# Two blocks of 256 tokens at a time in a fused attention and mixture-of-experts kernel: first products of 512 columns, and a new order of the opening

## The chip, the cores and the metric

One core of a Trainium2 chip runs the whole kernel. The metric is device time in microseconds for one execution; a time given without more is the median of several. A profiled execution also has a span, from its first to its last instruction. The engines are TensorE (PE in the rows; PEld is its loading of weights), VectorE (DVE), ScalarE (ACT), GpSimd (POOL) and SyncE (SP), which issues most of the DMAs. Each engine runs its own instructions in order and waits for others by semaphores.

## What is computed

```python
B, H, S, D = (4, 8, 576, 64)      # attention: scale, two causal masks, softmax, product with v
x = attention(q, k, v)            # laid out as x[2304, 512]
h = x @ w_in                      # first layer, w_in[512, 2048]
x1 = (h * np.cos(h)) @ w_out      # w_out[2048, 512]
logits = x1 @ w_gate + np.log1p(np.exp(x1 @ w_noise)) * noise     # 8 experts
top2_w = softmax of the two largest logits of each row
out[rows] += top2_w * (np.maximum(x1[rows] @ w1[e], 0) @ w2[e])   # w1[8, 512, 1024], w2[8, 1024, 512]
```

Four heads see the last 32 positions, four see every fourth of the last 128. The inputs of the first layer and of the experts come as 64-bit floats.

## The kernel before

Numbers are carried as two parts: a high part rounded to the type that TensorE multiplies at its full rate (float32r), and the rest, the low part. Each product of two numbers is three matmuls (PASSES, line 43: high x high, high x low, low x high). Splitting a tile into its parts is two operations: a copy on ACT that rounds, and a subtraction on DVE or POOL. For weights of the first layer three operations on DVE go ahead (w_bits, lines 323 to 325, tile `cut`), which cut a 64-bit float down to 32 bits; then w_parts (lines 331 and 333) makes the parts `wm`. The set OTHER names the subtractions that are on DVE and not on POOL (`w..` those of the weights, `g..` those of g below), and the moves that are on ACT.

The tokens are nine blocks of 256, the 2,048 hidden columns eight groups of 256. A step is one block and one group:

- g1 (line 595) multiplies the split x of the block, `xhl`, with the group's weights: 24 matmuls of 256 columns (2 halves of the group x 4 chunks x 3 passes; L606) into one of two banks `ph`;
- post (line 609) makes h cos h of it: ACT, DVE (L615), ACT Sin and Square (L617, L618), DVE (L619), then the parts of g: an ACT copy (L622) and a subtraction (L624);
- g2 (line 627) multiplies the g of two steps earlier with w_out: 12 matmuls of 512 columns (L634), which are added up over the groups in two of four banks `acc`.

The 72 steps: in steps 0 to 15 blocks 0 and 1 take turns, group by group, while the weights are still being loaded and split; then blocks 2 to 8 follow, eight steps each. `xhl` has two buffers, so the next block is split (x_split, line 586) while the present one is multiplied.

In between stands all other work, in an order written out by hand. LOADS and OPENING, two strings, give the opening: loads of queries, keys and values (Q, V) and of weights (W), scores (S), exponentials (E), norms (N: L511, L512 and the scaling), transposes (T), products with v (A), weight cuts (B) and parts (P), splits of x (X), first products (G). BESIDE, a table, gives the rest: a row `20:0` says what stands in step 20 at position 0. A step's positions are -1 (after g1), 0 and 1 (after the first half of g2), 2 (after its second half). There stand the later attention units (a_...), the weights (w_...), the splits of x, and the router of each block once its first layer is done (r_rows copies x1 out, r_trans turns it, r_gate, r_logits, r_exp, r_top, r_pick, r_rank, r_send choose the experts and send the rows). Routers take their banks from `acc`, attention from two banks `mid`. At the end of the steps the work of expert 0 begins (t_..., load_we, split_we). Then the expert stage follows: for each expert, w1 (L956) and w2 (L991).

## Time and profile before

| | us |
|---|---|
| median of three runs | 998.86 (997.47 to 1001.2) |
| the profiled execution | 999.23 |
| its span | 997.4 |
| TensorE busy | 966.2 (97%) |
| VectorE busy | 531.4 (53%) |
| ScalarE busy | 459.6 (46%) |
| GpSimd busy | 339.3 (34%) |
| mean granted clock of TensorE | 0.99 |

The shares are means over stages that differ: the opening, in which attention and the splitting of the weights run, up to some 130 us; the rest of the first layer with later attention units and the routers beside it, up to 538 us; and the expert stage. In a timeline a run of equal instructions is one row, with the start of the first, the time from there to the end of the last, and their number; since the end of a matmul is modelled and the next one starts before, the time that a group takes is read from its start to the start of the next group.

### The profile page before, as it was taken

The numbers are of one execution on the slowest core, as the hardware profiler recorded it, in microseconds if no ns is written. First come the engines' busy times: TensorE is split into PE (matmuls) and PEld (weight loads), VectorE is DVE, ScalarE is ACT, GpSimd is POOL, SyncE is SP. The second block draws the span as 40 slices with busy tenths as digits, with TensorE's granted clock in tenths as the row PEclk, the third lists the DMA queues.
The fourth block names the chain that finished last, engine by engine and source line by source line (L and its number), as shares of the span: only waits on it lengthen the run. The fifth ranks groups of instructions, "written<-read, shape, count | busy, mean of one in ns | idle before, by whom it ended". The sixth has DMA issues, their size and how long they took to land.

```text
span 997.4 us, 17303 instructions
## 1 busy us (share of the span) xinstructions
PE 966.2 (97%) x6843; PEld 848.6 (85%) x6843; DVE 531.4 (53%) x1151; ACT 459.6 (46%) x919; POOL 339.3 (34%) x457
## 2 busy tenths in 40 slices
PE   8798989999999999999999999999999999999996
PEld 5677879888888888898987789898898989898995
DVE  5899774546755555344466656354453535353321
ACT  6767665555646755465464435232332414232210
POOL 6634342343353342323332232332313232322302
PEclk9999989999999999999999999999999999999999
DMA  8843221312231210000064454443434243441201
GB/s 301 304 136 107 83 84 34 122 69 73 84 77 53 67 32 1 22 7 17 1 219 110 105 174 145 155 163 124 158 122 151 85 156 136 158 158 46 80 11 61
DMA packets 52596, 104.50 MB, mean 105 GB/s; under 512 B 12483, under 2 KB 24771, under 8 KB 52512
## 3 DMA queue, kind: packets, MB, share of 16 engines
q1 hardware_dynamic: 42528, 75.68, 23.3%
q0 software_dynamic: 9984, 27.68, 9.0%
q8 instruction: 55, 0.90, 0.4%
q14 instruction: 29, 0.24, 0.1%
HBM read 84.76 MB, written 19.59 MB: 105 GB/s over the span
## 4 chain that ended last, share of the span: by engine, by line
PE 80%; DVE 10%; ACT 4%; issue 2%; DMA 2%; POOL 1%; SPq 0%; DVEq 0%; POOLq 0%; ACTq 0%
PE pe L956 21%; PE ye L991 20%; PE ph L606 16%; PE acc L634 15%; PE sc L466 2%; DVE cut L324 2%; PE mo L549 2%; PE mgx L939 2%; DVE cut L325 2%; PE mt L529 1%; DVE cut L323 1%; DVE r L615 1%; DVE r L619 1%; DMA qts<-in_qT 1%; PE mx L661 1%
## 5 line engine op out<-in xcount | busy, mean ns | idle before, releaser
L606 PE MATMUL ph<-xhl,wm 128*128 128x256 f32 x1728 | 225.4, 286 | 6.6 <-POOL wm L333 3.1
L606 PEld LDWEIGHTS ph<-xhl,wm 128*128 128x128 f32 x1728 | 217.5, 193 | 14.2 <-POOL wm L333 4.2
L634 PE MATMUL acc<-wm,g 128*128 128x512 f32 x864 | 223.4, 401 | 5.2 <-ACT wm L331 2.0
L991 PE MATMUL ye<-we,h 128*128 128x512 f32 (+1 forms) x960 | 227.4, 393 | 0.0
L991 PEld LDWEIGHTS ye<-we,h 128*128 128x128 f32 (+1 forms) x960 | 172.7, 183 | 41.1
L634 PEld LDWEIGHTS acc<-wm,g 128*128 128x128 f32 x864 | 156.3, 190 | 38.0 <-ACT wm L331 2.4
L624 POOL TENSOR_TENSOR g<-r,g 128x512 fp32r<-128x512 f32 x65 | 84.3, 1298 | 183.3 <-ACT g L622 182.9
L956 PE MATMUL pe<-xga,we 128*128 128x352 f32 x768 | 126.1, 324 | 0.0
L956 PEld LDWEIGHTS pe<-xga,we 128*128 128x128 f32 x768 | 123.2, 188 | 0.4 <-issue 0.4
L1004 POOL DMA_INDIRECT out<-old,tir x35 | 35.3, 1008 | 219.9 <-DVE old L1002 215.5
L958 ACT ACTIVATE h<-pe 128x256 fp32r<-128x256 f32 (+1 forms) x128 | 54.3, 424 | 119.5 <-PE pe L956 119.5
L959 DVE SCALAR_TENSOR_TENSOR h<-pe,h 128x256 fp32r<-128x256 f32 (+1 forms) x128 | 60.6, 475 | 86.7 <-ACT h L958 83.2
L1002 DVE SCALAR_TENSOR_TENSOR old<-ye,wts,old 128x512 f32<-128x512 f32 (+1 forms) x35 | 26.2, 750 | 133.8 <-PE ye L991 133.8
L956 PE MATMUL pe<-xgb,we 128*128 128x256 f32 x768 | 90.1, 276 | 1.7 <-DVE h L959 1.7
L615 DVE SCALAR_TENSOR_TENSOR r<-r,ph 128x512 f32<-128x512 int32 x72 | 49.2, 683 | 78.5 <-ACT r L614 78.4
L956 PEld LDWEIGHTS pe<-xgb,we 128*128 128x128 f32 x768 | 88.8, 188 | 2.2 <-DVE h L959 1.9
L872 DVE TENSOR_TENSOR we<-wraw,we 128x512 fp32r<-128x512 f32 x128 | 88.0, 698 | 4.3 <-ACT we L871 1.7
L619 DVE SCALAR_TENSOR_TENSOR r<-r,ph 128x512 f32<-128x512 f32 x72 | 49.4, 686 | 70.4 <-ACT r L618 70.4
L871 ACT ACTIVATE we<-wraw 128x512 fp32r<-128x512 f32 x128 | 78.1, 623 | 0.0
L617 ACT ACTIVATE r<-r 128x512 f32<-128x512 f32 x72 | 45.5, 632 | 54.1 <-DVE r L615 53.9
L614 ACT ACTIVATE r<-ph 128x512 int32<-128x512 f32 x72 | 42.8, 595 | 56.4 <-PE ph L606 46.7
L622 ACT ACTIVATE g<-r 128x512 fp32r<-128x512 f32 x72 | 45.5, 632 | 48.4 <-DVE r L619 38.6
(191 smaller groups left out, 980.2 us busy)
## 6 DMA issues: line engine op xcount, KB each, us to landing
wraw<-in_we SPq DMA_DIRECT2D x64, 512.0 KB, 6.1
raw<-in_wm SPq DMA_DIRECT2D x28, 512.0 KB, 8.5
x1d<-x SPq DMA_DIRECT2D x9, 512.0 KB, 3.1
out<-zt SPq DMA_DIRECT2D x18, 256.0 KB, 4.2
vts<-in_v SPq DMA_DIRECT2D x11, 384.0 KB, 3.9
kts<-in_kT SPq DMA_DIRECT2D x13, 288.0 KB, 4.5
qts<-in_qT SPq DMA_DIRECT2D x13, 288.0 KB, 4.5
piece<-in_wm SPq DMA_DIRECT2D x4, 512.0 KB, 5.1
```

What stands on the lines that cost most here:

```text
L606: nc.tensor.matmul(ph[:, j, :], w[:, a, o:o + P], t[:, x, c, :], start=(c == 0 and n == 0 and (j == 0 or len(cs) == 4)), stop=(c == 3 and ...
L615: nc.vector.scalar_tensor_tensor(r, n, -TWO_PI, ph, op0=ALU.mult, op1=ALU.add)
L617: nc.scalar.activation(r, r, AF.Sin, scale=0.5)
L619: nc.vector.scalar_tensor_tensor(r, r, 0.5, ph, op0=ALU.subtract, op1=ALU.mult)
L624: eng.tensor_tensor(g[:, 1, :], r, g[:, 0, :].bitcast(F32), op=ALU.subtract)
L634: nc.tensor.matmul(ACC[blk][t], g[:, a, j * TB + t * P:j * TB + (t + 1) * P], w[:, x, 1024 + j * DM:1024 + (j + 1) * DM], start=(p == 0 an ...
L871: nc.scalar.activation(t[:, 0, fs], raw, AF.Copy)
L872: eng.tensor_tensor(t[:, 1, fs], raw, t[:, 0, fs].bitcast(F32), op=ALU.subtract)
L956: nc.tensor.matmul(ph[:, :n], w[:, a, o:o + P], x[:, b, c, :], start=(c == 0 and i == 0), stop=(c == 3 and i == 2))
L958: nc.scalar.activation(h[:, 0, f, :n], ph[:, :n], AF.Relu)
L959: nc.vector.scalar_tensor_tensor(h[:, 1, f, :n], ph[:, :n], 0.0, h[:, 0, f, :n].bitcast(F32), op0=ALU.max, op1=ALU.subtract)
L991: nc.tensor.matmul(acc, h[:, a, f, o:o + n], w[:, b, (f % 4) * DM:(f % 4 + 1) * DM], start=(f == 0 and i == 0), stop=(f == 7 and i == 2))
```

## The change

Blocks 0 to 7 are taken in pairs. A step is now one pair of blocks (512 tokens) and one half group (128 hidden columns): 64 such steps, f = 0 to 15 for each pair, and then block 8 with its eight steps as before. g1_pair has 12 matmuls of 512 columns (4 chunks x 3 passes), whose moving operand is 256 columns of the one block and 256 of the other. g2_pair has 12 matmuls of 512 columns, as g2, over four token tiles: it fills all four banks `acc` for a pair. `xhl` is one tile with a place for either block of a pair, no longer two rotating buffers. The routers of blocks 0 to 5 take their banks from `mid`. post is the same; a piece of w_out is one half group's, so w_parts(p,3) is needed one step later than w_parts(p,2).

```diff
+0:-1 w_load(3,0)
...
-12:-1 a_norm(7)
...
-20:0 r_rows(1) x_split(3)
...
+15:-1 x_split(2,0,2) w_parts(7,2) zero_out(5)
+15:0 x_split(3,0,2) x_split(3,2,4) x_split(2,2,3,1) x_split(2,3,4,1)
...
+31:-1 a_part(11,2) x_split(4,2,4) x_split(5,2,4) x_split(4,0,2) r_send(1,1)
+31:0 x_split(5,0,2)
...
+47:-1 x_split(6,0,2) x_split(7,0,2) x_split(7,2,4) x_split(6,2,4)
...
+63:-1 x_split(8)
...
-OTHER = set("g02 g04 g07 g10 g13 g14 g15 m40 m41 m50 m51 m60 m61 m70 m71 t62 t71 w02 w12 w20 w22 w32 w33 w42 w43 w53 w61 w63".split())
+OTHER = set("e4 e7 g0_0 g0_1 g0_10 g0_11 g0_14 g0_15 g0_2 g0_3 g0_4 g0_5 g0_6 g0_7 g0_9 m40 m50 m51 m60 m61 m70 m71 n2 t62 t70 t71 w02 w10 w11 w12 w20 w22 w32 w33 w41 w43 w50 w60 w61 w63 w73".split())
...
+    xhl = bpool.tile([P, 2, 2, 4, TB], F32R, name="xhl")
     XHL = {}
...
     def x_split(blk, c0=0, c1=4, st=2, eng=nc.vector):
-        if c0 == 0:
-            XHL[blk] = bpool.tile([P, 2, 4, TB], F32R, tag="xhl", name=f"xhl{blk}", bufs=2)
-        t = XHL[blk]
+        t = xhl[:, blk % 2]
+        XHL[blk] = t
...
+    def g1_pair(b, f, cs=range(4)):
+        w = WM[f // 2]
+        if (b, f) not in PH:
+            tag, bufs = ("acc", 4) if (b, f) == (0, 1) else ("ph", 2)
+            PH[b, f] = psum.tile([P, 2 * TB], F32, tag=tag, name=f"ph{b}_{f}", bufs=bufs)
+        ph = PH[b, f]
+        for c in cs:
+            for n, (a, x) in enumerate(PASSES):
+                o = c * 256 + (f % 2) * P
+                nc.tensor.matmul(ph, w[:, a, o:o + P], xhl[:, :, x, c, :],
+                                 start=(c == 0 and n == 0), stop=(c == 3 and n == 2))
+        return ph
...
+    def g2_pair(b, f, ts):
+        g, w = G[b, f], WM[f // 2]
+        if f == 0 and 0 in ts:
+            for blk in (b, b + 1):
+                ACC[blk] = [psum.tile([P, DM], F32, tag="acc", name=f"acc{blk}_{t}", bufs=4) for t in range(2)]
+        for t in ts:
+            for n, (a, x) in enumerate(PASSES):
+                nc.tensor.matmul(ACC[b + t // 2][t % 2], g[:, a, t * P:(t + 1) * P],
+                                 w[:, x, 1024 + f % 2 * DM:1024 + (f % 2 + 1) * DM],
+                                 start=(f == 0 and n == 0), stop=(f == 2 * NPAIR - 1 and n == 2))
+
...
+    def r_bank(blk, name):
+        tag, bufs = ("mid", 2) if blk < 6 else ("acc", 4)
+        return psum.tile([P, 512], F32, tag=tag, name=name, bufs=bufs)
...
-            if blk >= NBLK - 2:
+            if blk >= NBLK - 3:
...
-    steps = [(blk, p) for p in range(NPAIR) for blk in range(2)]
-    steps += [(blk, p) for blk in range(2, NBLK) for p in range(NPAIR)]
+    steps = [(b, f) for b in (0, 2, 4, 6) for f in range(2 * NPAIR)]
+    steps += [(NBLK - 1, p) for p in range(NPAIR)]
+    paired = range(64)
```

The strings LOADS and OPENING and most rows of BESIDE are new as well. Expert 0's first gathers read the rows of blocks 0 to 5 and no longer those of block 6, and a few tiles of the expert stage have other offsets. Three places show how the order moves.

VectorE in the first 15 us: L480 and L482 (L493 and L495 after) are the score reductions `sc` and `mx` of an attention unit, L511 and L512 (L524 and L525) its norm `sm`; the first number in a name is the unit. Before:

```order
L480 TENSOR_REDUCE sc1_1_230<-sc1_1_230 128x4
L482 TENSOR_SCALAR mx1_214<-sc1_1_230 128x4
L480 TENSOR_REDUCE sc2_0_254<-sc2_0_254 128x5
L482 TENSOR_SCALAR mx2_253<-sc2_0_254 128x5
L480 TENSOR_REDUCE sc2_1_268<-sc2_1_268 128x4
L482 TENSOR_SCALAR mx2_253<-sc2_1_268 128x4
L511 TENSOR_SCALAR sm0_242<-sm0_242 128x9
L512 RECIPROCAL sm0_242<-sm0_242 128x9
L534 COPY ahat_89<-mt0_0_298 96x384
L511 TENSOR_SCALAR sm1_282<-sm1_282 128x9
L512 RECIPROCAL sm1_282<-sm1_282 128x9
```

After:

```order
L493 TENSOR_REDUCE sc1_1_242<-sc1_1_242 128x4
L495 TENSOR_SCALAR mx1_226<-sc1_1_242 128x4
L524 TENSOR_SCALAR sm0_215<-sm0_215 128x9
L525 RECIPROCAL sm0_215<-sm0_215 128x9
L493 TENSOR_REDUCE sc2_0_270<-sc2_0_270 128x5
L495 TENSOR_SCALAR mx2_269<-sc2_0_270 128x5
L493 TENSOR_REDUCE sc2_1_284<-sc2_1_284 128x4
L495 TENSOR_SCALAR mx2_269<-sc2_1_284 128x4
L524 TENSOR_SCALAR sm1_254<-sm1_254 128x9
L525 RECIPROCAL sm1_254<-sm1_254 128x9
L547 COPY ahat_89<-mt0_0_301 96x384
L547 COPY ahat_89<-mt0_1_318 96x384
```

The norm of unit 0 stands ahead of the reductions of unit 2, and that of unit 1 behind them, ahead of the first copy of a transposed unit.

TensorE around steps 31 and 32, where the blocks change; in the names of after, the first number of ph, g and acc is the pair's first block or the block. Before:

```order
L634 MATMUL acc3_1_2632<-wm5_1260,g3_5_2986 128x512 x6
L466 MATMUL sc12_0_3201<-kts_83,qts_85 64x96 x10
L466 MATMUL sc12_1_3216<-kts_83,qts_85 64x96 x8
L606 MATMUL ph4_0_3228<-xhl4_3158,wm0_471 128x256 x24
L634 MATMUL acc3_0_2631<-wm6_1473,g3_6_3100 128x512 x6
L634 MATMUL acc3_1_2632<-wm6_1473,g3_6_3100 128x512 x6
L606 MATMUL ph4_1_3293<-xhl4_3158,wm1_559 128x256 x24
```

After:

```order
L629 MATMUL ph2_15_2715<-xhl_183,wm7_1428 128x512 x12
L562 MATMUL mo11_1_2728<-at11_1_2650,vts_84 64x32 x2
L562 MATMUL mo11_1_2728<-at11_1_2650,vts_84 64x64 x2
L562 MATMUL mo11_1_2728<-at11_2_2687,vts_84 64x64 x6
L669 MATMUL acc2_0_1775<-wm6_1346,g2_13_2635 128x512 x3
L669 MATMUL acc2_1_1776<-wm6_1346,g2_13_2635 128x512 x3
L479 MATMUL sc12_0_2767<-kts_83,qts_85 64x96 x10
L479 MATMUL sc12_1_2782<-kts_83,qts_85 64x96 x8
L669 MATMUL acc3_0_1777<-wm6_1346,g2_13_2635 128x512 x3
L669 MATMUL acc3_1_1778<-wm6_1346,g2_13_2635 128x512 x3
L629 MATMUL ph4_0_2803<-xhl_183,wm0_461 128x512 x12
```

VectorE at the same place, after:

```order
L637 SCALAR_TENSOR_TENSOR r2_14_2693<-r2_14_2693,ph2_14_2656 128x512
L641 SCALAR_TENSOR_TENSOR r2_14_2693<-r2_14_2693,ph2_14_2656 128x512
L579 COPY xraw_82<-mo11_1_2728 128x2x96
L579 COPY xraw_82<-mo11_1_2728 128x2x48
L605 TENSOR_TENSOR xhl_183<-xraw_82,xhl_183 128x512 x3
L637 SCALAR_TENSOR_TENSOR r2_15_2751<-r2_15_2751,ph2_15_2715 128x512
L605 TENSOR_TENSOR xhl_183<-xraw_82,xhl_183 128x512
L641 SCALAR_TENSOR_TENSOR r2_15_2751<-r2_15_2751,ph2_15_2715 128x512
```

Before, the split of block 4 (xhl4) stood in step 31 in a buffer of its own, and two scores stood ahead of the first product of block 4. After, the splits read what unit 11's products (mo11_1) give and write the tile that the products ph2_15 read, and ph4_0 stands eight rows behind ph2_15.

TensorE in step 66, in which the routers of blocks 6 and 7 begin, after (mx: transposes of x1, mg: gate products, ml: transposes of logits):

```order
L616 MATMUL ph8_2_4695<-xhl_183,wm2_725 128x256 x24
L656 MATMUL acc8_0_4723<-wm0_461,g8_0_4628 128x512 x6
L698 MATMUL mx6_0_4732<-ident_118,x1_6_4678 128x128 x4
L698 MATMUL mx6_1_4738<-ident_118,x1_6_4678 128x128 x4
L706 MATMUL mg6_4747<-x1t6_4731,wgn_170 32x256 x4
L698 MATMUL mx7_0_4755<-ident_118,x1_7_4691 128x128 x4
L698 MATMUL mx7_1_4761<-ident_118,x1_7_4691 128x128 x4
L656 MATMUL acc8_1_4724<-wm0_461,g8_0_4628 128x512 x6
L718 MATMUL ml6_4779<-ident_118,lp6_4752 128x128 x2
```

The gate product of block 6 stands behind its own two transposes; in the order of before first and second products stand between the transposes of a block and its gate.

## Rows read from the trace of the kernel before

**Rows 1.** Busy time by stretch: start:end, length, each engine (instructions), granted clock, DMA

```profile
20.00:135.00 115.00, 100.40 (x908) 84.71 (x907) 100.77 (x160) 78.02 (x196) 51.28 (x45) 0.94 0.43 148
125.00:150.00 25.00, 22.28 (x154) 19.37 (x151) 18.06 (x31) 17.41 (x42) 10.55 (x9) 0.86 0.30 84
150.00:200.00 50.00, 50.00 (x405) 44.57 (x400) 25.84 (x43) 28.58 (x50) 15.11 (x14) 1.00 0.25 82
```

**Rows 2.** Timeline of TensorE, steady stretch: start, us, engine, line, operation, names, count

```profile
155.84 2.91 PE L634 MATMUL acc<-wm,g 128*128 128x512 f32 x12
158.59 3.04 PE L606 MATMUL ph<-xhl,wm 128*128 128x256 f32 x24
161.46 2.91 PE L634 MATMUL acc<-wm,g 128*128 128x512 f32 x12
```

**Rows 3.** The chain of waits from 20 to 135 us, shares by line

```profile
by line: DVE cut L324 19.0%; DVE cut L325 13.0%; DVE cut L323 9.6%; issue 8.5%; ACT s L497 5.0%; DVE r L615 4.3%; DVE wm L333 3.9%; DVE r L619 3.3%; PE mo L549 3.0%; ACT wm L331 2.7%; PE ph L606 2.6%; PE acc L634 2.5%; DVE sc L480 2.4%; DVE
```

**Rows 4.** Timelines of ACT, VectorE and POOL in the first 23 us

```profile
9.42 0.24 ACT L497 ACTIVATION_READ_ACCUMULATOR s<-sc,mx 128x1 f32 x1
...
17.76 0.34 ACT L497 ACTIVATE ahead<-sc,mx 128x96 f32<-128x96 f32 x1 [2.30 <-DVE mx L482]
...
12.16 0.16 DVE L511 TENSOR_SCALAR sm<-sm 128x9 f32<-128x9 f32 x1
...
22.27 0.67 DVE L323 TENSOR_SCALAR cut<-raw 128x512 uint32<-128x512 uint32 x1
...
12.75 1.92 POOL L518 TENSOR_TENSOR s<-s,sm 128x288 f32<-128x288 f32 x3 [2.32 <-DVE sm L512]
```

**Rows 5.** Timeline of VectorE, 36 to 127 us; the last row is cut6_1

```profile
36.12 0.69 DVE L324 SCALAR_TENSOR_TENSOR cut<-raw,cut 128x512 uint32<-128x512 uint32 x1
...
39.64 0.69 DVE L615 SCALAR_TENSOR_TENSOR r<-r,ph 128x512 f32<-128x512 int32 x1 [1.58 <-ACT r L614]
...
45.27 1.66 DVE L325 SCALAR_TENSOR_TENSOR cut<-raw,cut 128x512 uint32<-128x512 uint32 x1
...
125.14 1.64 DVE L325 SCALAR_TENSOR_TENSOR cut<-raw,cut 128x512 uint32<-128x512 uint32 x1
```

**Rows 6.** Timeline of POOL at 45 us

```profile
44.97 1.41 POOL L624 TENSOR_TENSOR g<-r,g 128x512 fp32r<-128x512 f32 x1 [1.96 <-ACT g L622]
```

**Rows 7.** Groups by line, 20 to 135 us: busy us, mean ns, idle before

```profile
L324 DVE SCALAR_TENSOR_TENSOR cut<-raw,cut 128x512 uint32<-128x512 uint32 x28 | 26.1, 931 | 1.0
L325 DVE SCALAR_TENSOR_TENSOR cut<-raw,cut 128x512 uint32<-128x512 uint32 x28 | 24.0, 857 | 1.0
...
L333 DVE TENSOR_TENSOR wm<-cut,wm 128x512 fp32r<-128x512 f32 x10 | 7.1, 713 | 0.2
L624 DVE TENSOR_TENSOR g<-r,g 128x512 fp32r<-128x512 f32 x5 | 4.1, 816 | 0.6 <-ACT g L622 0.6
```

**Rows 8.** Timeline of TensorE, 102 to 135 us

```profile
114.84 1.55 PE L634 MATMUL acc<-wm,g 128*128 128x512 f32 x6
...
128.06 0.48 PE L455 MATMUL sc<-mask,identb 128*128 128x384 bf16 x1 [2.72 <-ACT xraw L566]
...
129.94 2.93 PE L634 MATMUL acc<-wm,g 128*128 128x512 f32 x6
132.67 3.66 PE L606 MATMUL ph<-xhl,wm 128*128 128x256 f32 x24
```

**Rows 9.** Groups by line, 140 to 500 us: the splits of x

```profile
L591 ACT ACTIVATE xhl<-xraw 128x512 fp32r<-128x512 f32 x13 | 7.6, 623 | 1.4 <-DVE xraw L566 1.4
...
L592 DVE TENSOR_TENSOR xhl<-xraw,xhl 128x512 fp32r<-128x512 f32 x13 | 9.3, 744 | 2.3 <-ACT xhl L591 2.3
```

**Rows 10.** Timeline of VectorE at 498 us: a router's copies

```profile
498.55 1.28 DVE L662 COPY x1t<-mx 128x512 f32<-128x512 f32 x2
```

**Rows 11.** Timeline of TensorE, 530 to 537 us

```profile
530.43 3.29 PE L634 MATMUL acc<-wm,g 128*128 128x512 f32 x12 [0.58 <-POOL g L624]
534.41 2.56 PE L634 MATMUL acc<-wm,g 128*128 128x512 f32 x10 [0.70 <-POOL spacer L764]
```

371 lines of the change are left out of this document (191 added, 180 removed), and 6 rows, old and new, of the table OPENING.

## The prediction

> **What bounds the kernel now.** I read first the busy time by stretch, then the timeline of TensorE in a steady stretch, then the chain of waits of the opening, then the same at the end of the first layer. From 150 us on TensorE is busy for the whole of every stretch [rows 1]: there the time is its matmuls, and only fewer or shorter matmuls make it shorter. A step there is 24 first products of 256 columns, 158.59 to 161.46, or 2.87 us, and 12 second products of 512 columns, 155.84 to 158.59, or 2.75 us [rows 2]: 119.6 and 229.2 ns from one start to the next. Before about 127 us it is another engine. The chain of waits from 20 to 135 us lies mostly on the bit cuts of VectorE: L324, L325 and L323 make up 42% of it [rows 3], and VectorE is busy for 100.77 of these 115 us [rows 1]. The cuts split the first layer's weights, and step i cannot start before the pieces of its hidden columns are split. So the opening is bound by VectorE and by the time at which its first cut can start (22.27 us), the rest by TensorE. The expert stage, from 538 us, keeps its instructions and order; I cost it at nothing.
>
> **The sum's base.** The profiled run took 999.23 us; 1.83 us of it lie outside the span, and it is 0.37 us above the median of the three runs, 998.86. I work in changes to the profiled run and take 0.37 off at the end.
>
> **Part 1: the product of 512 columns.** Of 64 steps each has 12 first products of 512 columns instead of 24 of 256. No first product of that width is in the trace; the nearest row is the second product, the same width, number and type with a weight load for each: 2.75 us against 2.87 [rows 2], 0.12 us a step. The new moving operand is two runs of 256 columns from two blocks instead of one run of 512. If that costs as much as two matmuls, the gain is nothing, and I take that as the other bound: no row gives a reason for a price above two matmuls, or for a gain above 0.12. Steps 0 to 11 run while VectorE is the bound, so theirs hides behind the cuts. 52 steps are left: 52 x 0.12 = **-6.2 us** (0 to -7.7, the latter with all 64).
> The Trainium skill (TensorE: Matmul & The Clock Gate, Back-to-back issue gap) gives a matmul that stands alone N/2.4 ns plus some 2.5 ns, so that halving the number would give only those 2.5 ns a pair. The rows do not agree: two of 256 cost 239.2 ns and one of 512 costs 229.2, 10 ns a pair. By the page's rule this term is -1.6 us.
>
> **Part 2: the opening.** Three things change.
> First, the head start. In the old order the first unit's sums (L511) stand on VectorE behind the score reductions of unit 2: ACT ends the exponentials of unit 0 at 9.66, L511 runs at 12.16, and POOL, idle for 2.32 us, begins to normalise at 12.75. Later ACT is idle for 2.30 us until the scores of unit 3 are there, at 17.76 [rows 4]. In the new order L511 and L512 of unit 0 stand ahead of unit 2's reductions, and the scaling of unit 2 goes to ACT. Unit 0's normalising can start about 9.66 plus the 0.59 us from L511 to POOL, some 10.3, or 2.5 earlier; the idle 2.30 on ACT goes in part. ACT has nine more operations for unit 2. By going down both queues I get the first cut at 19.4 instead of 22.27: **-2.9 us**. If ACT holds the chain up instead, it is nothing.
> Second, the subtractions. Up to step 12 eight more stand on VectorE: three of weight pieces and five of g. Two of the weights lie ahead of the first r (39.64 before), inside the head start; six are left, at 0.71 to 0.82 us: +4.5. Against that, VectorE is slowed while POOL subtracts: a cut of 0.69 us alone [rows 5] takes 1.66 when POOL's g runs beside it [rows 5, 6]. Over the opening the 28 cuts of L324 and of L325 have means of 931 and 857 ns [rows 7], 0.24 and 0.17 us above 0.69, 11.5 us in all. A POOL subtraction taken away thus gives back between nothing and 0.97 us; spread over POOL's 51.28 us of work there [rows 1], these 11.5 are 0.22 us for each us of POOL, or 0.3 for a subtraction of 1.41 [rows 6]. I count 0.5, as these subtractions lie among the cuts, while some of POOL's other work lies where VectorE is idle: -3.0.
> Third, each piece of w_out's second half is now needed half a weight group later, which takes one piece's three cuts, two of them 0.69 [rows 5], out of the way of each step: worth -1.5 where it is the last thing waited for. Together the second and third make 0 (-4 to +4.5). VectorE also idles in between, 115 - 100.77 us [rows 1], and I leave that as it is. The opening: **-2.9 us** (-7 to +4.5).
> Where the opening ends, TensorE waits 2.72 us for a bank that ACT frees, and then runs at a lower clock: 24 first products take 3.66 us instead of 3.04 [rows 2, 8] and 6 second products 2.93 instead of 1.55 [rows 8]; the granted clock of that stretch is 0.86 of full speed on average, so for a part of it the lower level of 1.2 GHz was granted, against 1.00, the 2.4 GHz, later [rows 1]. In the new order unit 7's scores stand at the same step behind the same copies; I leave it as it is.
>
> **Part 3: the seams.** The split x (xhl) is now one buffer for a pair of blocks, so the next pair can only be split between the last first product of one pair and the first of the next. An ACT copy takes 0.62 us and a VectorE subtraction 0.74 [rows 9]. E is the end of the pair's last first product.
> Step 31 to 32: unit 11's second half is multiplied after E, copied, then three splits follow, the post-processing's r, then the fourth. VectorE: E+0.5 +0.8 for the copies, 0.6 for ACT, 3 x 0.74, 0.69, 0.74: about E+5.4. TensorE has until then unit 11's 10 products, the second products of 2.75, and 18 score products, about 4.4. A wait of 1.0.
> Step 47 to 48: four splits at once, 4 x 0.62 + 0.74 = E+3.2 and a few tenths for hand-over; only 2.75 of second products cover it: 0.8. Step 63 to 64: two splits, E+2.0, covered by 2.75; if that cover went, it would cost 2.0. Step 15 to 16 is spread over several steps and covered.
> Step 18: the router's transposes of block 1 stand in the middle of the second products and wait for two ACT copies queued behind the post-processing: 0.5. Together **+2.3 us** (0 to +5).
>
> **Part 4: the end of the layer.** Blocks 6 and 7 end in the same step, so both their routers fall in steps 65 to 72, together with expert 0's loads and splits; before, block 6's was eight steps earlier. VectorE's share of a router there: two copies of 1.28 us together [rows 10] and a chain of small operations. In the new order the gate of block 6 stands on TensorE right behind its transposes, with nothing between, so TensorE waits for both copies: 1.0. The r of steps 68 and 69 queue behind the chain, and the second products of g two steps later wait: 1.7 and 0.8 by my count of the queue. Before, two waits of 0.58 and 0.70 stand there [rows 11]. 3.2 instead of 1.3: **+1.9 us** (0 to +4).
> Last, the routers of blocks 0 to 5 use the two banks that attention uses, no longer the four accumulators, which a pair fills. Where they meet, TensorE waits for a copy: **+0.3 us** (0 to +2).
>
> **Sum:** -6.2 - 2.9 + 2.3 + 1.9 + 0.3 = -4.6; 999.23 - 4.6 = 994.6, and with 0.37 off, **994.3 us**.
>
> **The rivals.**
> A, the opening gives more: VectorE's relief is nearer to 0.97 than to 0.5, or the wait of 2.72 us and the slow clock after it go with the new order (2.7 idle, 1.4 of slow second and 0.6 of slow first products, 4.7 in all). For it: the piece waited for there is one of the last attention units, and the whole order there is new. Against: the same copies stand before the same scores. 994.3 - 4.7 = 989.6 us.
> B, the opening grows, and the kernel is slower: the six or eight subtractions come to VectorE, which bounds the opening, at 0.70 us or more, nothing is given back because the cuts overlap other work of POOL, and the head start is lost to ACT's nine more operations. Place: VectorE from step 0 to step 11. Up to step 15 there are ten, four of weights and six of g: at 0.70 the opening is +7.0 instead of -2.9, 994.3 + 9.9 = 1004.2 us. It decides where relief stays under some 0.2 us each and the first cut is no earlier than 22.27.
> C, a first product whose moving operand lies in two runs costs as much as two of 256 columns, and the change of form brings nothing: 994.3 + 6.2 = 1000.5 us. For it: no such operand is in the trace. Against it: the number of columns, the type and the weight load are those of the second product, whose 229 ns the rows show.
> By the Trainium skill's rule of part 1 the same change of form would bring a little, 1.6 us, and the kernel would come out at 998.9; this trace's 10 ns a pair speak against it.
> D, waits at the seams, at the routers and at the end take the gain: they come to their upper bounds, 5 + 4 + 2 instead of 4.5: 994.3 + 6.5 = 1000.8 us. For it: one buffer, two shared banks, and a VectorE nearly full over the last eight steps.
>
> **How the numbers follow.** Forecast 0.43, A 0.21, B 0.12, C 0.08, D 0.16. A measurement of this kernel can tell 0.5%, 5 us, from no change: faster is under 993.9, slower over 1003.8. The forecast lies on that line; with its terms' scatter I give half of it to each side. Faster: 0.21 + A 0.21 = 0.42 or so. Slower: most of B, a little of D: 0.11. The rest, 0.47, is within 0.5%. The range, 987.5 to 1002.0, leaves out B and the third of A that lies below it (0.12 + 0.07).
>
> **What would show it.** Part 1: 12 first products of a pair take about 2.75 us from the first start to the next second product, anywhere in 150 to 500 us; at 2.87 C is right. Part 2: the first cut of VectorE at about 19.4 us, the first r at about 36.8, and the end of the cut of the second piece of group 6 (cut6_1) about three us earlier than now, 125.14 + 1.64 [rows 5]; if it comes later than now, B. Part 3: an idle time of TensorE of about 1 us before the first product of the third pair and of the fourth, ended by the splits on VectorE (line L592 in the code of before). Part 4: three idle times of TensorE in the last eight steps, together about 3 us. The prediction is wrong if the expert stage's length, 538 to 997, changes by more than 1 us, or if a new wait appears in steps 16 to 64 away from the seams.

## The result and the profile after

The changed kernel takes 985.47 us (median of five, 983.75 to 986.05); the kernel before, run beside it, 998.07 (five, 997.47 to 1001.2). The ratio is 0.9864, with a 95% interval of 0.9846 to 0.9883: 12.6 us less, where 994.3 was forecast and 987.5 was the low end of the range. The profiled execution of after took 984.7 us with a span of 983.0, 14.4 under the span of before: the execution shown of before lies 1.2 above its median of 998.07, that of after 0.8 below its own, so the traces show somewhat more than the times, 14.5 us instead of 12.6.

Where they went is read from one instruction that both kernels have in every step, ACT's first copy of the post-processing (L614 before, L636 after); the table gives its start in the two traces. A step holds the same amount of first and second products in both.

| step | before, us | after, us | difference | gained in the stretch | forecast for it |
|---|---|---|---|---|---|
| 0 | 39.01 | 36.98 | -2.0 | -2.0 | -2.9 |
| 12 | 136.43 | 130.85 | -5.6 | -3.6 | 0 |
| 16 | 161.66 | 152.90 | -8.8 | -3.2 | -0.5 |
| 66 | 495.26 | 477.98 | -17.3 | -8.5 | -3.2 |
| expert stage begins | 538.16 | 524.42 | -13.7 | +3.5 | +1.9 |
| end of the span | 997.4 | 983.0 | -14.4 | -0.7 | 0 |

The steady stretch, TensorE's timeline of after (columns as in rows 2):

```profile
382.69 2.88 PE L629 MATMUL ph<-xhl,wm 128*128 128x512 f32 x12
385.41 2.88 PE L669 MATMUL acc<-wm,g 128*128 128x512 f32 x12
388.13 2.88 PE L629 MATMUL ph<-xhl,wm 128*128 128x512 f32 x12
```

From start to start the 12 first products take 2.72 and the 12 second products 2.72 us, 5.44 together. Before it was 2.87 and 2.75 [rows 2]. So not one group became shorter but both: 0.15 and 0.03, 0.18 us a step. In the same trace block 8 keeps its 256 columns, and there the old numbers stand, 2.87 and 2.75:

```profile
463.61 3.04 PE L616 MATMUL ph<-xhl,wm 128*128 128x256 f32 x24
466.48 2.91 PE L669 MATMUL acc<-wm,g 128*128 128x512 f32 x12
469.23 3.04 PE L616 MATMUL ph<-xhl,wm 128*128 128x256 f32 x24
```

The opening, by stretch as in rows 1, and three rows of VectorE's timeline, the first cut, the first r and the last operation of cut6_1:

```profile
20.00:135.00 115.00, 100.88 (x749) 76.64 (x749) 101.14 (x167) 81.35 (x201) 38.27 (x36) 0.99 0.46 160
...
125.00:150.00 25.00, 24.40 (x144) 19.52 (x143) 19.77 (x34) 20.29 (x50) 9.93 (x10) 1.00 0.18 57
```

```profile
19.07 0.37 DVE L336 TENSOR_SCALAR cut<-raw 128x512 uint32<-128x512 uint32 x1
...
37.61 0.69 DVE L637 SCALAR_TENSOR_TENSOR r<-r,ph 128x512 f32<-128x512 int32 x1 [0.91 <-ACT r L636]
...
119.80 0.69 DVE L338 SCALAR_TENSOR_TENSOR cut<-raw,cut 128x512 uint32<-128x512 uint32 x1
```

VectorE is as full as before (101.14 of 115 us against 100.77), though it runs seven more instructions there; POOL has fallen from 51.28 to 38.27. The first cut begins at 19.07 instead of 22.27, the first r at 37.61 instead of 39.64, and cut6_1 ends at 120.49 instead of 126.78: VectorE's lead is 3.2, then 2.0, then 6.3 us. The granted clock of 125 to 150 us is 1.00 and no longer 0.86.

The end of the layer, the waits of TensorE from 478 us to the expert stage (waiting line, releaser, us in total, times, longest):

```profile
PE mg L706 <- DVE x1t L699: 1.5, 1, 1.5
PE acc L656 <- POOL spacer L801: 0.6, 1, 0.6
PE mgx L981 <- DVE xga L984: 0.5, 1, 0.5
PE mx L698 <- DVE x L683: 0.2, 1, 0.2
```

2.8 us, where before had 0.58, 0.70 and 0.17, or 1.45. The gate of block 6 does wait for the copies of x1, as forecast; no second product waits for g or r.

### The profile page after: what moved, and what is told of

Same layout as the page of the kernel before. It is cut to its first block, busy times and chain, and to the rows that moved or that the text cites. A ratio compares the mean times of both kernels' runs of the same rounds, so it can differ in the third digit from the quotient of the medians.

```text
span 983.0 us, 15767 instructions
## 1 busy us (share of the span) xinstructions
PE 951.4 (97%) x6075; PEld 801.1 (81%) x6075; DVE 532.5 (54%) x1163; ACT 460.4 (47%) x926; POOL 323.9 (33%) x444
## 4 chain that ended last, share of the span: by engine, by line
PE 78%; DVE 9%; ACT 7%; issue 2%; DMA 2%; POOL 1%; SPq 0%; ACTq 0%; DVEq 0%; POOLq 0%
PE pe L998 21%; PE ye L1033 21%; PE acc L669 14%; PE ph L629 13%; DVE cut L337 2%; PE sc L479 2%; PE mgx L981 2%; PE mo L562 1%; DVE cut L338 1%; PE ph L616 1%; ACT s L510 1%; DVE r L637 1%; PE mt L542 1%; DVE cut L336 1%; ACT r L639 1%
## 5 line engine op out<-in xcount | busy, mean ns | idle before, releaser
L669 PE MATMUL acc<-wm,g 128*128 128x512 f32 x768 | 196.2, 398 | 5.3 <-DVE r L641 2.2
L629 PE MATMUL ph<-xhl,wm 128*128 128x512 f32 x768 | 189.3, 393 | 6.1 <-POOL wm L346 3.4
L629 PEld LDWEIGHTS ph<-xhl,wm 128*128 128x128 f32 x768 | 142.6, 188 | 39.9 <-POOL wm L346 5.1
L669 PEld LDWEIGHTS acc<-wm,g 128*128 128x128 f32 x768 | 140.4, 188 | 35.8 <-DVE r L641 2.6
L646 POOL TENSOR_TENSOR g<-r,g 128x512 fp32r<-128x512 f32 x59 | 76.2, 1291 | 193.0 <-ACT g L644 189.5
L636 ACT ACTIVATE r<-ph 128x512 int32<-128x512 f32 x72 | 42.8, 594 | 40.6 <-PE ph L629 34.9
```

The costliest lines, as they stand in the source:

```text
L629: nc.tensor.matmul(ph, w[:, a, o:o + P], xhl[:, :, x, c, :], start=(c == 0 and n == 0), stop=(c == 3 and n == 2))
L646: eng.tensor_tensor(g[:, 1, :], r, g[:, 0, :].bitcast(F32), op=ALU.subtract)
L669: nc.tensor.matmul(ACC[b + t // 2][t % 2], g[:, a, t * P:(t + 1) * P], w[:, x, 1024 + f % 2 * DM:1024 + (f % 2 + 1) * DM], start=(f == 0 a ...
```

## The experiments

### The form of the product, and the opening in three parts

Each kernel was timed beside the kernel before, in four sittings, in which that kernel's medians were 998.07 (after), 998.23 (two256, old_new_opening, old_subs, hold_clock), 997.46 (seam_bare, gate_late, w51, all_subs) and 997.06 us (the three with "copy" in the name, and best). Differences between kernels of two sittings are good to a microsecond or two; the ratio of each is to its own sitting. Of the code only the lines or names that change are shown; three points stand for the rest.

**two256**: the changed kernel, with each first product of a pair as two of 256 columns.

```diff
-                nc.tensor.matmul(ph, w[:, a, o:o + P], xhl[:, :, x, c, :],
-                                 start=(c == 0 and n == 0), stop=(c == 3 and n == 2))
+                for h in range(2):
+                    nc.tensor.matmul(ph[:, h * TB:(h + 1) * TB], w[:, a, o:o + P], xhl[:, h, x, c, :],
+                                     start=(c == 0 and n == 0 and h == 0), stop=(c == 3 and n == 2),
+                                     skip_group_check=True)
```

> The changed kernel with one edit: each first product of a pair is made as two products of 256 columns with the same weights, one for each block; order, buffers and seams stay. Theory P (what the form of the product is worth is 0.18 us a step, 5.62 to 5.44, wherever TensorE bounds): if the opening is VectorE's, steps 12 to 63 lose 52 x 0.18 = 9.4 and the time is 985.5 + 9.4 = 994.9 us; if TensorE bounds part of the opening too, up to 64 x 0.18 = 11.5, 997.0. Rival (the gain of the change is its order and the loads spread over VectorE and POOL, and the product only the 0.12 of the prediction): 985.5 + 6.2 = 991.7 or less.

Measured: 994.8 us, ratio 0.9968 (0.9957 to 0.9978). The form is worth 994.8 - 985.5 = 9.3 us by the medians, as much as 52 steps of 0.18. The traces show less of it in the steps. From step 0 to step 12 the two kernels take 93.89 and 93.87 us, so up to there the form counts for nothing: the prediction's cover of steps 0 to 11 was right. From step 12 to the expert stage this one falls 7.4 us behind, 0.18 in each step in which TensorE has nothing else to do and 0.14 on average over 52; the other 1.3 of the 9.0 us between the spans lies in the expert stage, which is the same in both (459.9 and 458.6 us; in all the traces 458.1 to 460.1). Its steady rows settle where the 0.03 of the second products comes from:

```profile
388.26 3.04 PE L630 MATMUL ph<-xhl,wm 128*128 128x256 f32 x24
391.13 2.91 PE L671 MATMUL acc<-wm,g 128*128 128x512 f32 x12
393.88 3.04 PE L630 MATMUL ph<-xhl,wm 128*128 128x256 f32 x24
```

The second products are those of the changed kernel, four token tiles and all, and take 2.75 again. They are shorter only where 512-column products stand around them.

**old_new_opening**: the kernel before with the new strings LOADS and OPENING.

```diff
 LOADS = (
-    "Q0 Q1 Q2 V0 Q3 V1 V2 W00 V3"
+    "Q0 Q1 V0 Q2 Q3 V1 V2 V3 W00"
...
 OPENING = (
-    "W01 S0 S1 E0 C0 S2 Q4 E1 N0 W02 T00 N1 T01 C1 E2 S3 T11 T10 W10 C2 E3 T02 N2 A00 T12 W11 A10a A01a "
...
+    "W02 C0 S0 E0 S1 E1 N0 S2 N1 T00 C1 C2 E2 T01 W01 S3 E3 Q4 C3 T10 N2 T11 A00 T12 T02 A10 W10 W11 "
...
-OTHER = set("g02 g04 ...
+OTHER = set("n2 g02 g04 ...
```

> The kernel before with one part of the change: the new strings LOADS and OPENING, and unit 2's scaling on ACT; steps, products and the rest of the order stay as before. Theory O (the opening's gain is the order ahead of step 0, the head start): the first r comes 2 to 3 us earlier than 39.0 and the whole kernel with it, 998.1 - 2.5 = 995.6 us. Rival (it is lost again in steps 0 to 11, where VectorE and TensorE wait for each other, and the gain needs the new steps): the first r earlier, step 12 at the old time, 998 us.

Measured: 994.68 us, ratio 0.9966 (0.9954 to 0.9977): 3.5 us. In its profiled execution, the slowest of its seven, the lead is 1.0 at step 0 and between 1.5 and 1.9 from step 1 to step 12. The order ahead of step 0 pays for itself, and the lead is not lost in steps 0 to 11.

**old_subs**: the changed kernel with the old assignment of the subtractions of steps 0 to 15.

```diff
# OTHER, the names g and w of steps 0 to 15:
-g0_0 g0_1 g0_10 g0_11 g0_14 g0_15 g0_2 g0_3 g0_4 g0_5 g0_6 g0_7 g0_9
+g0_1 g0_4 g0_7 g0_8 g0_9 g0_11 g0_14
...
-w02 w10 w11 w12 w20 w22 w32 w33 w41 w43 w50 w60 w61 w63 w73
+w02 w12 w20 w22 w32 w33 w42 w43 w53 w61 w63
```

> The changed kernel with the old assignment of the subtractions: 7 of the 16 g of steps 0 to 15 and 11 weight pieces on VectorE as before, the others on POOL. Theory S0 (the prediction's step: cost and relief cancel): within 1.5 us of 985.5. Theory S+ (the relief of VectorE from POOL is a main part of the opening's gain, 0.97 us for a subtraction of 0.7): eight of them back cost 8 x 0.27 = 2 us and POOL's longer subtractions, 1.4 us in place of 0.7, another 0.7 where one is waited for: 988 to 992 us. Rival S- (they burden VectorE): 2 to 4 us faster than 985.5.

Measured: 988.8 us, ratio 0.9909 (0.9891 to 0.9926), 3.3 us over the changed kernel. At step 12 it is 2.8 us ahead of the kernel before and the changed kernel 5.6, and both began within 0.05 us of each other: the other half of the lead is the subtractions. From step 0 to step 12 this kernel takes 96.71 us and old_new_opening, which has the old steps, 96.66: with the old subtractions the new steps, the later need for the pieces of w_out among them, bring nothing there. The groups of VectorE from 20 to 135 us (columns as in rows 7), first the changed kernel, then this one:

```profile
L338 DVE SCALAR_TENSOR_TENSOR cut<-raw,cut 128x512 uint32<-128x512 uint32 x28 | 21.7, 774 | 1.0
L337 DVE SCALAR_TENSOR_TENSOR cut<-raw,cut 128x512 uint32<-128x512 uint32 x28 | 21.6, 772 | 1.0
L336 DVE TENSOR_SCALAR cut<-raw 128x512 uint32<-128x512 uint32 x27 | 12.0, 444 | 0.6 <-POOL wm L346 0.6
L346 DVE TENSOR_TENSOR wm<-cut,wm 128x512 fp32r<-128x512 f32 x14 | 10.2, 730 | 0.8 <-ACT wm L344 0.6
L646 DVE TENSOR_TENSOR g<-r,g 128x512 fp32r<-128x512 f32 x11 | 9.6, 872 | 1.4 <-ACT g L644 1.4
```

```profile
L337 DVE SCALAR_TENSOR_TENSOR cut<-raw,cut 128x512 uint32<-128x512 uint32 x28 | 25.5, 911 | 1.0
L338 DVE SCALAR_TENSOR_TENSOR cut<-raw,cut 128x512 uint32<-128x512 uint32 x28 | 23.6, 842 | 1.0
L336 DVE TENSOR_SCALAR cut<-raw 128x512 uint32<-128x512 uint32 x27 | 14.2, 527 | 1.7 <-POOL wm L346 1.7
L346 DVE TENSOR_TENSOR wm<-cut,wm 128x512 fp32r<-128x512 f32 x11 | 8.2, 744 | 0.9 <-ACT wm L344 0.6
L646 DVE TENSOR_TENSOR g<-r,g 128x512 fp32r<-128x512 f32 x6 | 4.7, 785 | 0.1
```

Eight more subtractions cost VectorE 10.2 - 8.2 + 9.6 - 4.7 = 6.9 us and give its cuts back 3.9 + 1.9 + 2.2 = 8.0: one us for each, not the half that was counted.

**all_subs**: the changed kernel with every subtraction of steps 0 to 15 on VectorE.

```diff
# OTHER, the names that are added:
+g0_8 g0_12 g0_13 w00 w01 w03 w13 w21 w23 w30 w31 w40 w42 w51 w52 w53 w62 w70 w71 w72
```

> The changed kernel with all subtractions of steps 0 to 15 on VectorE (16 of g and all of the weight pieces), none on POOL. By the groups of the changed kernel and of the one with the old assignment, eight subtractions moved to VectorE cost it 6.9 us and gave its cuts back 8.1. Theory L (that holds only as long as cuts are still slowed: what is left above their undisturbed 0.69 and 0.42 us is 5.3 us, and 16 more subtractions in the opening cost 16 x 0.73 = 11.7): step 16 comes 4 to 7 us later and the kernel takes 989 to 992 us. Rival (each one moved is a gain): 983 us or less.

Measured: 989.39 us, ratio 0.9921 (0.9904 to 0.9937), 3.9 us over the changed kernel. Step 16 comes 4.4 us later, 2.1 of it already at step 0. The cuts are nearly undisturbed now, and nothing more is to be had from them:

```profile
L337 DVE SCALAR_TENSOR_TENSOR cut<-raw,cut 128x512 uint32<-128x512 uint32 x28 | 20.1, 719 | 1.0
L338 DVE SCALAR_TENSOR_TENSOR cut<-raw,cut 128x512 uint32<-128x512 uint32 x28 | 19.7, 704 | 1.0
```

Of the two other assignments that were tried both lose, the one with fewer and the one with all.

### The wait ahead of unit 7's scores, and the clock behind it

**hold_clock**: the kernel before, with TensorE kept busy in the wait of 2.72 us [rows 8] by products with a tile of zeros.

```diff
+    zw = cpool.tile([P, P], BF, name="zw")
+    nc.vector.memset(zw, 0.0)
...
+            if f is a_scores and a == (7,):
+                for _ in range(12):
+                    nc.tensor.matmul(ACC[0][0][:, :480], zw, masks[1][:, 0:5, :], start=False, stop=False,
+                                     skip_group_check=True)
```

> The kernel before with 12 more products with a weight tile of zeros, added to an open sum, ahead of the scores of unit 7, where TensorE waits 2.72 us; nothing else changes. Theory C (the lower clock after that wait costs time): the stretch from 125 to 135 us, granted 0.72 and 0.59 before, is near 1.00; 6 second products take 1.55 us instead of 2.93 and 24 first 3.04 instead of 3.66, step 16 comes 2 us earlier and the kernel takes 996 us. Rival (something else bounds there, or the clock falls for another reason): the clock stays low, or step 16 comes when it did: 998 to 999 us.

The clock did what theory C says, the time did not. In the profile the two stretches are granted 1.00, six second products take 1.65 us and step 16 comes 1.1 us earlier (1.4 when the later start of this execution is taken off). Stretches 125 to 130 and 130 to 135 us of hold_clock:

```profile
125.00:130.00 5.00, 4.55 (x50) 2.81 (x49) 4.90 (x7) 2.45 (x6) 1.65 (x2) 1.00 0.00 0
130.00:135.00 5.00, 5.00 (x35) 4.61 (x34) 4.79 (x11) 4.64 (x16) 1.10 (x1) 1.00 0.11 16
```

But the timed runs give 997.77 us against 998.23, a ratio of 0.9999 (0.9990 to 1.0009). A part of the gain goes again in the profile itself, in a wait of 0.88 us for a load of values at 148.59 that the kernel before does not have.

**w51**: the changed kernel with one more subtraction, piece 1 of group 5, on VectorE.

```diff
# OTHER, the names of group 5:
-w50 w60
+w50 w51 w60
```

> The changed kernel with one more subtraction, that of piece 1 of group 5, on VectorE, where POOL has a scaling and a g ahead of it and TensorE waits 2.27 us for it at 108 us. Theory Q (the wait is POOL's queue): the wait is gone, step 16 comes 1.5 to 2.3 us earlier and the kernel takes 983.5 us. Rival (another piece, or VectorE's cuts, is the next late thing): under 0.7 us gained, 985 us.

Measured: 987.42 us, ratio 0.9907 (0.9885 to 0.9929): slower than the changed kernel. Neither theory foresaw it. The wait of 2.27 us is gone, and step 10 comes 0.8 us earlier although this execution began 0.4 later. But the wait ahead of unit 7's scores grew from 1.26 to 2.56 us; behind it 16 score products take 1.55 us instead of 0.88 and six second products 2.93 instead of 1.65, and step 16 comes 2.2 us later. TensorE's timeline, the scores in the changed kernel and then w51:

```profile
121.77 0.32 PE L468 MATMUL sc<-mask,identb 128*128 128x384 bf16 x1 [1.26 <-ACT xraw L579]
```

```profile
122.02 0.48 PE L468 MATMUL sc<-mask,identb 128*128 128x384 bf16 x1 [2.56 <-ACT xraw L579]
122.43 1.55 PE L479 MATMUL sc<-kts,qts 64*64 64x96 f32 x16
123.90 2.93 PE L669 MATMUL acc<-wm,g 128*128 128x512 f32 x6
```

What is waited for there is told by ACT's timeline of the kernel before. The copy that frees the bank (L566) stands in ACT's queue behind the copy of a weight piece (L331), and that waits for VectorE's cut6_1, which ends at 126.78 [rows 5]:

```profile
126.81 0.63 ACT L331 ACTIVATE wm<-cut 128x512 fp32r<-128x512 f32 x1 [2.10 <-DVE cut L325]
127.34 0.66 ACT L566 COPY xraw<-mo 128x96 f32<-128x96 f32 x2
```

**before_copy**, **early_copy** and **w51_copy** take ACT's copy out from behind it, in the kernel before, in the changed one and in w51. The rows of the first are shown; in the other two `w_parts(6,1)` and `a_part(6,2)` change places in row 11:-1.

```diff
-10:2 w_bits(6,0) w_bits(6,1) w_parts(6,0) w_bits(6,2) w_parts(6,1)
-11:-1 a_part(6,2)
+10:2 w_bits(6,0) w_bits(6,1) w_parts(6,0) w_bits(6,2)
+11:-1 a_part(6,2) w_parts(6,1)
```

> The kernel before with one exchange: ACT's copy of unit 6's second half, which frees the bank for the scores of unit 7, stands ahead of ACT's copy of weight piece 1 of group 6, no longer behind it; that copy waits for VectorE's cut until 126.8 us. Theory W (the wait of 2.72 us at 128 us is VectorE's cut, handed on by ACT's queue, and the lower clock follows from its length): the bank is free 1.9 to 2.7 us earlier, the wait is under 0.9 us, the granted clock from 125 to 135 us is 1.00, step 16 comes 2.5 to 4.5 us earlier, and the kernel takes 994 to 996 us. Rival (steps 12 to 16 are bound by the weight pieces of group 7 behind it): the clock stays up, but step 16 comes less than 1 us earlier: 997 to 998 us.

> The changed kernel with the same exchange: the copy of unit 6's second half ahead of that of weight piece 1 of group 6. Theory W: the wait of 1.26 us ahead of unit 7's scores is gone, and nothing else changes: 984.3 us. Rival: the weights of groups 6 and 7 are next: 985.5 us.

> The changed kernel with the subtraction of piece 1 of group 5 on VectorE and that exchange together. The first alone took the wait of 2.27 us at 108 us away, but the wait ahead of unit 7's scores grew from 1.26 to 2.56 us and the granted clock behind it fell to 0.50. Theory W: with the exchange that wait stays under 0.9 us, the clock stays at 1.00, and the gain of step 10 (1.5 us) is kept: 983.0 to 984.0 us. Rival (VectorE has no room, and the next weight piece takes it back): 985.5 us or more.

In before_copy the wait shrinks to 0.15 us, the clock of 125 to 135 us is 1.00, and step 16 comes 2.5 us earlier in the profile, 0.5 of which is an earlier start. The 2.57 us of wait do not go for good: the next products wait for VectorE instead, 0.21 us and then 1.28, and two more waits of 0.27 and 0.42 us follow up to 148 us, none of which the kernel before has.

```profile
124.96 0.32 PE L455 MATMUL sc<-mask,identb 128*128 128x384 bf16 x1 [0.15 <-ACT xraw L566]
...
135.06 3.13 PE L606 MATMUL ph<-xhl,wm 128*128 128x256 f32 x24 [1.28 <-DVE r L619]
```

The timed runs again show nothing: 996.77 us against 997.06, ratio 0.9996 (0.9986 to 1.0005).

early_copy takes 985.48 us (ratio 0.9882, 0.9856 to 0.9907), and this does not decide between its two theories. Its four times are 984.09, 984.32, 986.63 and 988.3: the first two are theory W's 984.3. The wait is gone from its profile, which is the execution of 986.63, but that need not be the edit. At step 10, ahead of the edit, this execution lost 1.5 us against the changed kernel's trace, behind a wait that both have: there the lower clock followed, in the changed kernel it did not. TensorE then came to the scores late by more than the wait had been. From step 0 to step 11 the two take 84.47 and 84.54 us, to step 16 116.27 and 115.92: no gain shows. TensorE in the changed kernel, then in early_copy:

```profile
108.46 1.20 PE L629 MATMUL ph<-xhl,wm 128*128 128x512 f32 x4 [2.27 <-POOL wm L346]
```

```profile
110.32 2.07 PE L629 MATMUL ph<-xhl,wm 128*128 128x512 f32 x4 [2.24 <-POOL wm L346]
```

w51_copy takes 984.31 us (0.9867, 0.9851 to 0.9884): with the exchange w51's loss is gone, the wait is 0.78 us and the clock behind it stays at 1.00. The gain of step 10 is not kept, though; it comes back as a wait for VectorE, and step 16 comes at 153.10, in the changed kernel at 152.90:

```profile
130.08 3.04 PE L629 MATMUL ph<-xhl,wm 128*128 128x512 f32 x12 [1.69 <-DVE r L641]
```

**again1** and **again2**, the kernel before in two more profiled executions, were to tell why two kernels gain in their profile and not in their times.

> The kernel before, unchanged, in another profiled execution. Two kernels that keep the clock up at 125 to 135 us took 1.2 to 3.1 us less in their profiled execution than the one shown of before, and the same in the timed ones. Theory V (the lower clock there comes in some executions only, and the one shown was one of the slower): in at least one of two further executions the stretch from 125 to 135 us is granted near 1.00, the wait of some 2.7 us still stands there, and the time is 996 to 998 us. Rival (it is in every execution, and the gain of the two kernels is lost elsewhere when they are not profiled): 0.72 and 0.59 in both, 999 us.

> The same as again1, in a third execution: by theory V at 1.00 in one of the two, by the rival 0.72 and 0.59 in both.

Both took the wait, 2.88 us, and both the lower clock, but not alike. The stretches 125 to 130 and 130 to 135 us, again1 and then again2:

```profile
125.00:130.00 5.00, 2.12 (x32) 1.62 (x33) 4.86 (x8) 2.73 (x6) 1.44 (x1) 0.78 0.00 0
130.00:135.00 5.00, 5.00 (x27) 4.20 (x24) 4.79 (x11) 4.37 (x15) 1.27 (x1) 0.54 0.04 6
```

```profile
125.00:130.00 5.00, 2.49 (x21) 1.88 (x21) 4.90 (x9) 2.97 (x7) 1.92 (x2) 0.90 0.00 0
130.00:135.00 5.00, 5.00 (x30) 4.62 (x30) 4.67 (x9) 4.97 (x21) 0.04 (x1) 0.76 0.25 65
```

Theory V in its strict form falls, the clock was at 1.00 in neither; but in again2 the loss is half of that in the others, and it reached step 16 1.7 us before the execution shown, of which 0.7 is its start. So what the lower clock costs differs from one execution to the next by about 1 us, and by the two intervals taking the wait or the clock away gains at most 1.4 us in the median. Most of the gap between profile and times is the scatter of single executions. Of the 3.1 us between the spans of before and before_copy 0.5 is the start and 0.7 the expert stage, which the edit does not touch. From step 10 to step 16 the three executions of before take 46.6, 46.7 and 45.6 us, hold_clock 45.2 and before_copy 44.6: gains of 0.5 to 1.5 and of 1.0 to 2.0. There are too few profiled executions to say which of these the medians contain.

### The seam and the end

**seam_bare**: the changed kernel with the scores of unit 12 taken out of step 31 (here they read the queries and keys that are already loaded for unit 13, so the result is another; the amount of work is the same).

```diff
-31:1 a_scores(12)
-32:-1 a_exp(12)
+32:1 a_scores(12)
...
-33:-1 a_loadv(12)
+33:-1 a_exp(12) a_loadv(12)
```

> The changed kernel with the scores of unit 12 moved from step 31 to step 32, so that 36 score products, 1.63 us on TensorE, no longer stand ahead of the third pair's first product. Theory K (the seam costs nothing because it is covered: the splits end 5.15 us after the pair's last first product, and TensorE has 5.45 us of other work until then): now the cover is 3.8, and TensorE waits 1.2 to 1.5 us ahead of the third pair's first product, for a split on VectorE. Rival (the splits would be early anyway, the prediction's count of VectorE's queue was too long): no wait or under 0.5 us. The kernel's time by K: 985.5 to 987.0 us.

In the changed kernel TensorE comes to the third pair's first product, at 262.86, without a wait, 0.30 us after VectorE's fourth split has ended (TensorE, then VectorE):

```profile
257.41 0.80 PE L562 MATMUL mo<-at,vts 96*64 96x32 f32 x20
258.14 1.66 PE L669 MATMUL acc<-wm,g 128*128 128x512 f32 x6
259.74 1.70 PE L479 MATMUL sc<-kts,qts 64*64 64x96 f32 x36
261.37 1.65 PE L669 MATMUL acc<-wm,g 128*128 128x512 f32 x6
262.86 2.88 PE L629 MATMUL ph<-xhl,wm 128*128 128x512 f32 x12
```

```profile
261.88 0.68 DVE L605 TENSOR_TENSOR xhl<-xraw,xhl 128x512 fp32r<-128x512 f32 x1
```

Without the scores as cover it waits twice:

```profile
261.35 0.51 PE L628 MATMUL ph<-xhl,wm 128*128 128x512 f32 x1 [0.36 <-issue]
262.44 2.78 PE L628 MATMUL ph<-xhl,wm 128*128 128x512 f32 x11 [0.58 <-DVE xhl L604]
```

0.94 us of waiting, 0.58 of it put down to VectorE's split and 0.36 to nothing that the profile shows; from step 36 on every step comes some 1.35 us later than in the changed kernel, and its one execution took 987.24 us. Theory K holds, with a wait a little under its 1.2. At this seam the single buffer costs nothing because it is covered, by 0.3 us, and the cover can be lost.

**gate_late**: the changed kernel with the gate of block 6 behind the transposes of block 7.

```diff
-66:1 r_gate(6) r_trans(7)
-66:2 load_we(0,0,0) ...
+66:1 r_trans(7)
+66:2 r_gate(6) load_we(0,0,0) ...
```

> The changed kernel with the gate product of block 6 behind the transposes of block 7 and the second half of the second products of step 66, no longer directly behind its own transposes. Theory R (the 1.47 us in which TensorE waits for the copies of x1 in step 66 are on the path): that wait is gone or under 0.3 us and the kernel is 1.0 to 1.5 us faster, 984.2 us. Rival (VectorE is nearly full over the last eight steps, and the wait comes back at a later second product or router product): the expert stage starts when it did, 985.5 us.

Measured: 985.15 us, ratio 0.9875 (0.9859 to 0.9892), the same as the changed kernel. The 1.47 us came back as 0.35 and 0.55 at the next things that VectorE makes:

```profile
482.17 0.66 PE L698 MATMUL mx<-ident,x 128*128 128x128 f32 x4 [0.35 <-DVE x1t L699]
...
485.60 0.44 PE L718 MATMUL ml<-ident,lp 128*128 128x128 f32 x2 [0.55 <-DVE lp L711]
```

From step 66 to step 71 it gains 0.5 us on the changed kernel. **best** has it together with w51_copy's edits.

> The one before, and the gate product of block 6 behind the transposes of block 7 as well, which alone gave nothing clear (its 1.47 us of wait came back as 0.35 and 0.55). Theory: 0.5 us under the one before, 982.5 to 983.5 us. Rival: the same as the one before.

Measured: 983.9 us, ratio 0.9863 (0.9847 to 0.9880). Beside w51_copy it is 0.4 us less, within both spreads, and its ratio is that of the changed kernel, 0.9864: by these runs it does not beat it.

## Why the prediction was wrong

The path was right: VectorE's cuts bound the opening and TensorE's products the rest. The steps that failed are three terms of the sum: the price of a product of 512 columns, the relief that a moved subtraction gives VectorE, and the cover of the seams. All three were set too dear, and the kernel came out below the range.

**Part 1, 52 x 0.12 = -6.2: the mechanism right, the size not.** In a step in which TensorE has nothing else to do it is 0.18; two256 measured 9.3 in the medians, and 7.4 in the traces up to the expert stage. The working took the second product of before as the price of a 512-column product. That row, 2.75 us, is one of a group between two groups of 256 columns, and holds 0.03 us that the neighbours cause; a group among its like takes 2.72. The same 0.03 was missed a second time, as the second products of the pair gain it too. A pair of 256-column products costs 239 ns, one of 512 columns 226.7. The lower bound, a gain of nothing, is contradicted. By the rule of the Trainium skill (TensorE: Matmul & The Clock Gate, Back-to-back issue gap) a pair would have saved 2.5 ns and the kernel an estimated 1.6 us. The trace does not agree, with 12.5 ns a pair.

**Part 2, the head start, -2.9: right in kind.** The first cut was forecast at 19.4 and began at 19.07. Of its 3.2 us the first r kept 2.0: forecast at 36.8, it began at 37.61. The start of step 0 differs between executions, from 38.28 to 39.63 in the five traces with the old opening, so a row of one trace cannot settle 0.9 us. In the medians the order alone is worth 3.5 us.

**Part 2, the subtractions, 0: a step that failed.** The range given for the relief was nothing to 0.97 us for each, and 0.5 was taken. It is 1.0, the upper end, which was the one row with both engines side by side [rows 5, 6]. The mean that pulled it down was taken over all of POOL's work; that much of this work lay beside an idle or short-running VectorE is likely, and not shown. With relief at 1.0 and a price of 0.86 a subtraction is a small gain for VectorE; and what waits for it has it in 0.7 instead of 1.4 us. Together -3.3 by old_subs, and 2.8 in the traces at step 12. The third item in this zero, -1.5 for the later need of a piece of w_out, shows nowhere: with the old subtractions the new steps bring nothing up to step 12. So the zero was made of two errors, a relief too small and a gain that did not come.

**The stretch at 128 us, left as it was: wrong in the profile, small in the times.** The same copies do stand before the same scores, but the copy waits behind a weight piece for VectorE's cut. cut6_1 ends 6.3 us earlier and TensorE comes to these scores only 4.8 us earlier (120.51 after, 125.34 before, each the start of the late product less its wait), so the wait fell by 1.5 to 1.26 us, and the clock stayed up. That is rival A's mechanism. Its 4.7 us were read off one execution and took it that nothing waits behind; in before_copy 2.2 us of other waits came in, and the two kernels that take the wait or its clock out of before gain at most 1.4 in the median.

**Part 3, the seams, +2.3: wrong, nothing.** At 31 to 32 VectorE's queue was right (E+5.4 forecast, though its terms add up to 5.55; E+5.15 measured, with E at 257.41), the cover not: 18 score products were counted where 36 run, and 10 products with v where 20 run; the cover is 5.45 us and not 4.4. One row of the order stood for two matmuls, one for each of two heads. At 47 to 48 two of the four ACT copies ran before the last product had ended (from 367.93; the product runs from 366.23 to 369.09), since they write the half tile whose last readers were through, and the other two began at 369.29; the forecast had them all start at E. VectorE's last split ended at 371.24, and the next pair's first product started at 371.81 without a wait. Nor did TensorE wait for the router's transposes of step 18, for which 0.5 stood.

**Part 4, the end, +1.9: one wait right, the rest by luck.** The three waits forecast, 1.0, 1.7 and 0.8, add up to 3.5 and not to the 3.2 that was used. The first came, 1.47 us where it was forecast. The two of second products behind VectorE's r did not come; the one second product that waited, 0.62, waited for POOL's spacer, as one did before for 0.70, and a transpose of expert 0's rows waited 0.53 for VectorE. In all the waits grew by 1.35 us. Of the rest of the +3.5 in the table some 1.7 is the router of block 6, TensorE's work that stood before step 66 and now stands behind it (0.85 + 0.57 + 0.14 + 0.14 for its second transposes, gate, logits and ranks); 0.5 stays open.

**The whole.** Each of the three gains, taken alone, is 9.3, 3.5 and 3.3 us by the medians, 16.1 together, and the kernel gained 12.6. Against them stand the 1.35 us of waits at the end and, from 150 to 478 us, five short waits of 1.56 us in all where before had 0.73, or 0.8 more. These five are what the prediction had named as a sign of being wrong. The other 1.3 us are not accounted for; the parts were measured in different surroundings and need not add up, and the traces, which give 7.4 where the medians give 9.3, divide them otherwise. Three terms came out better than forecast together, by 3.1 (the product), 3.3 (the subtractions) and 2.3 us (the seams); 994.3 less these 8.7 is 985.6. That this meets the measured 985.47 is partly luck, as the smaller misses of the other terms cancel. The range had room below for one of the three at a time, as rival A, and not for all. The rivals B, C and D did not come.

## What to carry to other kernels

Price a matmul from a group that stands among its like, and when a group's neighbours change width, price the neighbours again. When two engines slow each other, take the row that shows both side by side, not a mean over a stretch, for a piece of work that is moved from one to the other; and expect the gain to end where the disturbed instructions are back at their undisturbed time. Before taking a wait away, look up in the queue of the engine that releases the next one what it stands behind: in w51 a wait of 2.27 us went, and a longer one with a lower clock behind it took its place. And count what waits behind the wait: in before_copy 2.57 us went and 2.2 us came back, in w51_copy 1.69.
